# Routing attention with a gated feed-forward on one core: the cluster masks of the later steps on VectorE, and weight chunks loaded two ahead

## The chip, the core and the metric

The kernel runs on one core of a Trainium2 chip. A core has five engines with instruction streams of their own: TensorE (PE), which multiplies matrices out of SBUF into the banks of PSUM, VectorE (DVE), ScalarE (ACT), GpSimd (POOL) and SyncE (SP), which here issues the transfers. They wait for each other by semaphores alone, and each works its own stream in order. The metric is the device time of one execution in microseconds (us), the median over several runs.

## What is computed

The reference has two parts. Attention with a mask by clusters, for 4 batches and 8 heads of 768 positions and 64 features:

```python
q_assign = np.argmax(np.einsum('bhsd,hcd->bhsc', q_n, c_n), axis=-1)   # 16 clusters
k_assign = np.argmax(np.einsum('bhsd,hcd->bhsc', k_n, c_n), axis=-1)
mask = q_assign[:, :, :, None] == k_assign[:, :, None, :]
scores = scale * np.matmul(q, k.transpose(0, 1, 3, 2))
scores = np.where(mask, scores, -1000000000.0)
...
attn = attn / (np.sum(attn, axis=-1, keepdims=True) + 1e-09)
return np.matmul(attn, v).astype(np.float32)
```

Its result, as 3072 tokens of 512 features, goes through a feed-forward with 2048 hidden units:

```python
h = x @ w_in
relu6 = np.clip(h + 3.0, 0.0, 6.0)
g = h * relu6 / 6.0
return (g @ w_out).astype(np.float32)
```

The weights come as 64-bit floats; the kernel makes 32-bit ones of them.

## The kernel before

Two heads make a pair, 16 pairs in all (g = 0 to 15). A pair has 12 steps: two halves of the queries (hf) times six chunks of 128 keys (j). So there are 192 steps, numbered n; `where(n)` gives (g, hf, j). A batch is 4 pairs, 48 steps.

**One step.** `scores` (L425) writes, for both heads, keys by queries into a tile ps of two PSUM banks (two such tiles, L147). `scores_part` (L414) issues two matmuls, one for each head, first with the one-hot clusters xm (bf16; the keys' one-hots are inverted and scaled by -2^60, so that pairs of different clusters get -2^60), then with xf, the transposed queries and keys in fp32, which add the products. An fp32 matmul is two PE instructions in the profile, a bf16 one is one. At the first step of a pair xf goes first. `exponentials` (L438) is one ACT instruction from ps to ex in SBUF; `key_sums` (L456) adds ex to acc on POOL; `attn_v` (L468) multiplies by the values into pv, over six steps, and copies pv out to num. `divide` (L486) sums acc over the keys by a matmul with ones into pd, takes its reciprocal on DVE (L499), multiplies num (L500) and sends num to DRAM (L503), from where the feed-forward reads it. pd, like other small PSUM tiles (`scratch`, L174), is in the pool psum_t, which has one buffer from step 96 on.

**Masks on VectorE.** `masks`, `clusters`, `spread` and `by_vector` (L373 to L454) are a second way, for pairs from MASKED on. MASKED is 16 (L169), the number of pairs, so it is never taken.

**Preparing a pair.** `turn` (L303) transposes q and k in three parts, `cluster_scores` (L319) and `route` (L330) find the clusters (L337 and L343 on DVE), `route_turn` (L361) transposes the one-hots into xm. `prep_items` (L785) spreads this over the 12 steps of the pair before.

**Weights.** There are 32 chunks (L205 to L256). `load_weights` (L205) loads one into a raw tile (two buffers, L144); `decoding_steps` (L210) has five steps: split, join, power, rest and total, with two ACT instructions (L221, L237) and five on DVE (L225 to L252). split of chunk i asks for chunk i + 1 (L215); rest (L247) reads raw last. `share` (L815) says how many decoding steps follow each pair of steps. They run until about step 96.

**Feed-forward.** `ffn_items` (L602) has, for each block of 256 tokens, eight up items and seven down items. An up item (`halved`, L650) is a form with seven products instead of eight: PE writes three products into uX and four into uY (both from the pool psum_m with two buffers, L150), DVE adds them up (L669, L676), ACT lifts (L523), and DVE clips (L526) one item later (`finish`, L634). Every second item POOL makes sums of the gates (L648). A down item is eight matmuls of 256 (16 PE instructions, L693), with a few additions on DVE (L700).

**The order of the work.** The instructions stand in each engine's stream as the code issues them (`manual_schedule`, L879); nothing is reordered. The loop (L898) takes two steps at a time; r = n mod 12. Until step 96 each pair of steps is followed by values of earlier steps, preparation, decoding, and from step 60 on a few up items. From step 96 on (DECODED) the function `four_by_four` (L842) works four steps together: at r = 0, 4 and 8 two steps are followed by the values of four earlier steps, at r = 2, 6 and 10 by a slot of feed-forward items and preparation. `items_by` (L821) sets how many items are issued up to a step: four or five a slot. `divide` comes at r = 4 ahead of the values (for the second half of the pair before) and at r = 8 in the midst of the values (L865 to L871). `later` and `checks` defer small work: num's transfer and the range sums on ACT (L512, L513) are issued in the pair of steps after.

The items in the slots from step 118 on, U for up and D for down: 118 UUUU, 122 UUUU, 126 DDDDD, 130 DDUU, 134 UUUUU, 138 UDDD, 142 DDDDU, 146 UUUU, 150 UUUD, 154 DDDDD, 158 DUUU, 162 UUUUU, 166 DDDD, 170 DDDU, 174 UUUUU, 178 UUDD, 182 DDDDD, 186 UUUU.

## Time and profile before

| what | value |
| --- | --- |
| median of 8 runs | 1014.46 us (1012.98 to 1018.86) |
| the profiled execution | 1016.26 us, of them 1014.4 us span |
| mean granted TensorE clock | 0.996 |
| busy share of the span: PE, DVE, ACT, POOL | 98%, 56%, 38%, 42% |
| score matmuls with xm (L418, bf16) | 384 instructions, 61.0 us busy |
| score matmuls with xf (L418, fp32) | 768 instructions, 157.0 us busy |
| reciprocals (L499) | 32, mean 2557 ns |
| bytes read from and written to HBM | 75.79 MB, 15.73 MB |

How to read the profile: it is one execution, recorded by the hardware, and all times in it are counted from the span's start. The span is from the first to the last instruction; the time of an execution has a little around it. PE is the matmul itself, PEld the load of its weights, which runs beside other matmuls. Matmuls overlap: the next begins before the last has drained, so the distance from start to start tells what one costs. A group line gives an engine, an operation, what it writes and reads with shapes, the number of instructions, their busy time and mean, and then the time that the engine was idle just ahead of them and who ended it. A timeline line has the start, the length, the engine and the group; in brackets is the idle time ahead of it. An arrow "<-" before an engine's name means "released by".

The trace can be cut by what the loop does. The first exponentials of the pairs stand at 15.0 us (pair 0), 111.9 (4), 139.7 (5), 244.2 (8, step 96), 313.8 (9), 380.6 (10, step 120), 717.6 (15); from 785 us on there is only feed-forward.

### The profile page before, as it was taken

What the parts mean: (1) busy time and instruction counts of PE and PEld (TensorE: products, weight loads), DVE (VectorE), ACT (ScalarE), POOL (GpSimd) and SP (SyncE); (2) the same over time, 40 slices, a digit from 0 to 9 for tenths busy, and PEclk for the clock granted to TensorE, in tenths of its full rate; (3) what the DMA queues carried; (4) which work ended last, traced back from release to release, by engine and by line L of the source; (5) the groups of instructions that cost most, each with busy time, mean ns of one, the idle gap of its engine ahead of it and who ended that gap; (6) DMA issues with size and microseconds to landing.
All of it is one profiled execution on the core that took longest, in us unless ns stands there. A gap on an engine that the chain in (4) does not pass through costs nothing.

```text
span 1014.4 us, 16735 instructions
## 1 busy us (share of the span) xinstructions
PE 991.0 (98%) x6560; PEld 736.4 (73%) x6560; DVE 564.5 (56%) x1085; ACT 390.4 (38%) x764; POOL 430.7 (42%) x363
## 2 busy tenths in 40 slices
PE   8999999999999999999999999999999999999996
PEld 4444445555688777788787777778777899999995
DVE  4788888988855255236336237147156372727270
ACT  6788877665233233234323333333223020201010
POOL 3877766665416326426415426515426130303030
PEclk9999999999999999999999999999999999999998
DMA  6344455532253052223223225123023041414120
GB/s 177 104 114 135 127 164 146 138 116 59 102 167 86 9 144 78 55 78 88 72 84 99 47 68 135 28 76 102 21 91 92 31 144 39 128 51 117 53 63 25
DMA packets 87560, 92.70 MB, mean 91 GB/s; under 512 B 53936, under 2 KB 68272, under 8 KB 87472
## 3 DMA queue, kind: packets, MB, share of 16 engines
q1 hardware_dynamic: 87328, 91.51, 31.9%
q8 instruction: 54, 0.88, 0.4%
q14 instruction: 34, 0.28, 0.1%
q10 hardware_dynamic: 144, 0.03, 0.0%
HBM read 75.79 MB, written 15.73 MB: 90 GB/s over the span
## 4 chain that ended last, share of the span: by engine, by line
PE 87%; DVE 6%; ACT 4%; DMA 1%; issue 1%; SPq 0%; ACTq 0%; DVEq 0%
PE Y L693 16%; PE uY L658 15%; PE ps L418 13%; PE X L693 12%; PE uX L658 12%; PE pv L474 11%; PE pqk L310 2%; PE pd L495 2%; PE ph L613 2%; PE pcs L323 1%; DVE tx L580 1%; DMA raw<-in_moe_w_out_dram 1%; ACT ex L441 1%; PE po L367 1%; DVE rcp L499 1%
## 5 line engine op out<-in xcount | busy, mean ns | idle before, releaser
L464 POOL TENSOR_TENSOR acc<-acc,ex 128x768 f32<-128x768 f32 x128 | 241.8, 1889 | 132.3 <-ACT ex L441 125.6
L648 POOL TENSOR_TENSOR g_sb<-g_sb 128x256 f32<-128x256 f32 x176 | 127.5, 746 | 319.3 <-DVE g_sb L526 298.1
L441 ACT ACTIVATE ex<-ps 128x768 f32<-128x768 f32 x192 | 148.4, 805 | 85.0 <-PE ps L418 84.5
L523 ACT ACTIVATE sx<-g_sb,half_c 128x512 f32<-128x512 f32 x88 | 63.6, 722 | 268.3 <-DVE g_sb L669 268.3
L418 PE MATMUL ps<-xf 64*128 64x384 f32 x768 | 157.0, 487 | 0.8 <-ACT ex L441 0.8
L474 PE MATMUL pv<-ex,vt 128*64 128x384 f32 x768 | 141.1, 496 | 0.0
L700 DVE TENSOR_TENSOR y<-y,Y 128x256 f32<-128x256 f32 x48 | 20.2, 420 | 169.9 <-PE Y L693 169.1
L474 PEld LDWEIGHTS pv<-ex,vt 128*64 128x64 f32 x768 | 48.7, 136 | 82.4 <-issue 72.7
L499 DVE RECIPROCAL rcp<-pd 128x384 f32<-128x384 f32 x32 | 81.8, 2557 | 47.7 <-PE pd L495 46.8
L461 POOL TENSOR_TENSOR acc<-ex 128x768 f32<-128x768 f32 x32 | 59.6, 1864 | 100.8 <-ACT ex L441 100.7
L658 PE MATMUL uX<-xb,w_in_sb 128*128 128x128 f32 x704 | 93.0, 275 | 0.0
L693 PE MATMUL X<-w_out_sb,g_sb 128*128 128x256 f32 x384 | 90.6, 384 | 0.0
L693 PE MATMUL Y<-T,g_sb 128*128 128x256 f32 x384 | 87.3, 380 | 0.0
L693 PE MATMUL Y<-w_out_sb,g_sb 128*128 128x256 f32 x384 | 87.2, 380 | 0.0
L658 PEld LDWEIGHTS uX<-xb,w_in_sb 128*128 128x128 f32 x704 | 85.7, 192 | 0.0
L418 PEld LDWEIGHTS ps<-xf 64*128 64x128 f32 x768 | 67.7, 188 | 21.7 <-issue 18.0
L693 PEld LDWEIGHTS X<-w_out_sb,g_sb 128*128 128x128 f32 x384 | 71.9, 192 | 13.8 <-issue 4.1
L693 PEld LDWEIGHTS Y<-T,g_sb 128*128 128x128 f32 x384 | 72.3, 190 | 11.2 <-issue 1.7
L693 PEld LDWEIGHTS Y<-w_out_sb,g_sb 128*128 128x128 f32 x384 | 72.2, 190 | 11.1 <-issue 1.1
L526 DVE SCALAR_TENSOR_TENSOR g_sb<-sx,g_sb 128x512 f32<-128x512 f32 x88 | 67.3, 770 | 0.9 <-ACT sx L523 0.9
L418 PE MATMUL ps<-xm 64*128 64x384 bf16 x384 | 61.0, 327 | 6.4 <-ACT ex L441 3.3
L669 DVE TENSOR_TENSOR g_sb<-uY,sx 128x128 f32<-128x128 f32 (+1 forms) x176 | 65.6, 414 | 0.1
(110 smaller groups left out, 1383.4 us busy)
## 6 DMA issues: line engine op xcount, KB each, us to landing
tx<-td SPq DMA_DIRECT2D x86, 384.0 KB, 3.2
raw<-in_moe_w_in_dram SPq DMA_DIRECT2D x16, 512.0 KB, 3.9
raw<-in_moe_w_out_dram SPq DMA_DIRECT2D x16, 512.0 KB, 3.6
qk<-in_q_dram SPq DMA_DIRECT2D x32, 192.0 KB, 4.3
qk<-in_k_dram SPq DMA_DIRECT2D x32, 192.0 KB, 4.7
vt<-in_v_dram SPq DMA_DIRECT2D x32, 192.0 KB, 3.8
xd<-num SPq DMA_DIRECT2D x32, 192.0 KB, 3.0
xb<-xd SPq DMA_DIRECT2D x12, 512.0 KB, 4.1
```

The lines of the kernel that those rows point to most:

```text
L418: nc.tensor.matmul(st["ps", n][:, t, 0:HALF], lhsT=x[r, NCH + j], rhs=x[r, hf * NHC : (hf + 1) * NHC], start=first, stop=last,)
L441: nc.scalar.activation(out=ex, in_=sc, func=ACT.Exp, scale=SM_SCALE)
L461: nc.gpsimd.tensor_tensor(out=acc, in0=st["ex", n - 1], in1=ex, op=ALU.add)
L464: nc.gpsimd.tensor_tensor(out=acc, in0=acc, in1=ex, op=ALU.add)
L474: nc.tensor.matmul(pv[t * D : (t + 1) * D], lhsT=vt[:, t, j], rhs=ex[:, t], start=(j == 0), stop=(j == NCH - 1),)
L499: nc.vector.reciprocal(out=rcp, in_=pd)
L523: nc.scalar.activation(out=r, in_=h, func=ACT.Relu, bias=half_c, scale=1.0 / 6.0)
L526: nc.vector.scalar_tensor_tensor(out=g, in0=r, scalar=1.0, in1=h, op0=ALU.min, op1=ALU.mult)
L648: eng.tensor_tensor(out=out_, in0=in0, in1=in1, op=op)
L658: nc.tensor.matmul(dst, lhsT=w[:, kt], rhs=x(kt), start=(kt == 0), stop=(kt == HK - 1))
L669: nc.vector.tensor_tensor(out=out_, in0=in0, in1=in1, op=ALU.add)
L693: nc.tensor.matmul(bank[:, half * HC : (half + 1) * HC], lhsT=g_sb[:, kind, i], rhs=w[:, i], start=(first and i == 0), stop=(last and i == ...
```

## The change

Pairs 10 to 15 (steps 120 to 191) now take the second way, and that way is another: `masks` writes 0 or -2^60 with a `tensor_scalar` on DVE straight into the banks of ps, out of xm (which now holds each query's cluster number on every partition) and the key's cluster number kid; PE then adds the score products onto it. The two masks of a step are written as soon as the exponentials two steps earlier have left the banks: at r = 0, 4 and 8 for the next two steps, four masks at once, ahead of the reciprocal; at r = 2, 6 and 10 singly, two behind a feed-forward item, from the first item on at r = 2, from the second on at r = 6 and 10. `clusters` now gives the numbers of queries and keys by two multiplications, one reduction and one copy, at the end of the slot at r = 6; `spread` transposes each number, repeated 128 times, in two parts instead of three. At r = 2, 6 and 10 the key sums follow their exponentials at once. The division is split: `sum_up` issues pd's matmuls right behind the last values of a half (r = 0 and 8, no longer r = 4 and 8), and the reciprocal and the multiplication follow at the end of that pair of steps. Only the division of step 95 stays at r = 4. Chunks are asked for two ahead, with three raw buffers, and `share` has one step more at r = 2 in the first part and one less at r = 4 in the second.

The diff, cut where only names or the index of `number` change:

```diff
@@ -141,7 +141,7 @@
     dram = pool("dram", 1, space=bass.MemoryType.DRAM)
     yp = pool("yp", 1)
     decoding = ctx.enter_context(ExitStack())
-    rawp = decoding.enter_context(tc.tile_pool(name="rawp", bufs=2))
+    rawp = decoding.enter_context(tc.tile_pool(name="rawp", bufs=3))
     decp = decoding.enter_context(tc.tile_pool(name="decp", bufs=2))
     startp = decoding.enter_context(tc.tile_pool(name="startp", bufs=1))
     psum_s = pool("psum_s", 2, space=PSUM)
@@ -166,7 +166,7 @@
     counts = const.tile([P, 2, NPAIR], F32, name="counts")
     w_low = const.tile([P, 1], F32, name="w_low")
-    MASKED = NPAIR
+    MASKED = NPAIR // 2 + 2
     st = {}
     later = []
     numbers = []
@@ -212,7 +212,7 @@
         got = {}
         def split():
-            load_weights(i + 1)
+            load_weights(i + 2)
             raw = st.pop(("raw", i))
             got.update(lo=raw[:, :, 0], hi=raw[:, :, 1])
             got["size"] = decp.tile([P, WC], BF16, name="wsize")
@@ -356,7 +357,7 @@
         later.append(count)
         if g >= MASKED:
-            numbers.append(lambda: clusters(g))
+            numbers.extend(clusters(g))
     def route_turn(g, part):
         if part == 0:
@@ -374,33 +375,36 @@
         return where(n)[0] >= MASKED
     def clusters(g):
-        oh = one_hot.rearrange("p j (t c) -> p j t c", t=2)[:, :, :, 0:C]
-        which = rtp.tile([P, NC2, 2, C], BF16, name="which")
-        nc.vector.tensor_tensor(
-            out=which, in0=oh, in1=number.unsqueeze(1).unsqueeze(1).to_broadcast([P, NC2, 2, C]), op=ALU.mult
-        )
+        oh = one_hot.rearrange("p (h j) (t c) -> p h j t c", h=2, t=2)[:, :, :, :, 0:C]
+        which = rtp.tile([P, 2, NCH, 2, C], BF16, name="which")
         qid = st["qid"] = rtp.tile([P, NCH, 2], BF16, name="qid")
-        kid = st["kid", g] = kidp.tile([P, NCH, 2], F32, name="kid")
-        nc.vector.tensor_reduce(out=kid, in_=which[:, NCH:], axis=AX.X, op=ALU.add)
-        nc.vector.tensor_scalar(
-            out=kid, in0=kid, scalar1=-1.0, scalar2=C * (C - 1) / 2.0, op0=ALU.mult, op1=ALU.add
-        )
-        qsum = rtp.tile([P, NCH, 2], F32, name="qsum")
-        nc.vector.tensor_reduce(out=qsum, in_=which[:, 0:NCH], axis=AX.X, op=ALU.add)
-        nc.vector.tensor_copy(out=qid, in_=qsum)
-    def spread(g, part):
-        if part == 0:
+        kid = st["kid", g] = kidp.tile([P, 2, NCH, 2], F32, name="kid")
+        def weigh():
+            for h in range(2):
+                nc.vector.tensor_tensor(
+                    out=which[:, h], in0=oh[:, h],
+                    in1=number[:, h].unsqueeze(1).unsqueeze(1).to_broadcast([P, NCH, 2, C]), op=ALU.mult,
+                )
+        def collect():
+            nc.vector.tensor_reduce(out=kid, in_=which, axis=AX.X, op=ALU.add)
+        def narrow():
+            nc.vector.tensor_copy(out=qid, in_=kid[:, 0])
+        return [weigh, collect, narrow]
+    def spread(g, t):
+        if t == 0:
             st["xm", g] = xp.tile([P, NC2, P], BF16, name="xm")
-        pb = scratch([P, 4, P], "pb")
-        for i in range(4):
-            t, j = divmod(4 * part + i, NCH)
-            nc.tensor.matmul(
-                pb[:, i], lhsT=st["qid"][:, j, t : t + 1].to_broadcast([P, P]), rhs=ident_q,
-                start=True, stop=True,
-            )
-        nc.scalar.copy(out=st["xm", g][:, 4 * part : 4 * part + 4], in_=pb)
+        pb = scratch([P, NCH, P], "pb", BF16)
+        for j in range(NCH):
+            nc.tensor.transpose(
+                out=pb[:, j], in_=st["qid"][:, j, t : t + 1].to_broadcast([P, P]), identity=ident_q
+            )
+        nc.scalar.copy(out=st["xm", g][:, t * NCH : (t + 1) * NCH], in_=pb)
     def where(n):
@@ -409,48 +413,53 @@
     def scores_qk(n):
         st["ps", n] = psum_s.tile([P, 2, 512], F32, name="ps")
-        scores_part(n, st["xf", where(n)[0]], True, by_vector(n))
-    def scores_part(n, x, first, last):
+        scores_part(n, st["xf", where(n)[0]], True, False)
+    def scores_part(n, x, first, last, onto=False):
         g, hf, j = where(n)
         for t in range(2):
             r = slice(t * D, (t + 1) * D)
             nc.tensor.matmul(
                 st["ps", n][:, t, 0:HALF], lhsT=x[r, NCH + j],
                 rhs=x[r, hf * NHC : (hf + 1) * NHC], start=first, stop=last,
+                skip_group_check=onto,
             )
     def scores(n):
         g, hf, j = where(n)
+        if by_vector(n):
+            scores_part(n, st["xf", g], False, True, True)
+            return
         if ("ps", n) not in st:
-            if hf == j == 0 or by_vector(n):
+            if hf == j == 0:
                 scores_qk(n)
             else:
                 st["ps", n] = psum_s.tile([P, 2, 512], F32, name="ps")
                 scores_part(n, st["xm", g], True, False)
                 scores_part(n, st["xf", g], False, True)
                 return
-        if not by_vector(n):
-            scores_part(n, st["xm", g], False, True)
+        scores_part(n, st["xm", g], False, True)
     def exponentials(n):
         sc = st.pop(("ps", n))[:, :, 0:HALF]
         ex = st["ex", n] = expp.tile([P, 2, HALF], F32, name="ex")
         nc.scalar.activation(out=ex, in_=sc, func=ACT.Exp, scale=SM_SCALE)
-    def masks(n):
+    def masks(n, heads=(0, 1)):
         g, hf, j = where(n)
-        if not by_vector(n):
+        if n >= total or not by_vector(n):
             return
-        ex = st["ex", n]
-        for t in range(2):
-            nc.vector.scalar_tensor_tensor(
-                out=ex[:, t].rearrange("p (a b) -> p a b", b=P),
+        if ("ps", n) not in st:
+            st["ps", n] = psum_s.tile([P, 2, 512], F32, name="ps")
+        for t in heads:
+            nc.vector.tensor_scalar(
+                out=st["ps", n][:, t, 0:HALF].rearrange("p (a b) -> p a b", b=P),
                 in0=st["xm", g][:, t * NCH + hf * NHC : t * NCH + (hf + 1) * NHC],
-                scalar=st["kid", g][:, j, t : t + 1], in1=ex[:, t].rearrange("p (a b) -> p a b", b=P),
-                op0=ALU.is_equal, op1=ALU.mult,
+                scalar1=st["kid", g][:, 1, j, t : t + 1], scalar2=-FAR,
+                op0=ALU.not_equal, op1=ALU.mult,
             )
     def key_sums(n):
@@ -484,6 +493,9 @@
     def divide(n):
+        return sum_up(n)()
+    def sum_up(n):
         g, hf, _ = where(n)
         b, kt = divmod(g, NKT)
         if kt == 0 and hf == 0:
@@ -495,17 +507,21 @@
             nc.tensor.matmul(
                 pd[t * D : (t + 1) * D], lhsT=ones, rhs=acc[:, t], start=True, stop=True
             )
-        rcp = nump.tile([P, HALF], F32, name="rcp")
-        nc.vector.reciprocal(out=rcp, in_=pd)
-        nc.vector.tensor_tensor(out=num, in0=num, in1=rcp, op=ALU.mult)
-        def keep():
-            nc.sync.dma_start(st["xd", b][:, kt, hf * HALF : (hf + 1) * HALF], num)
-            in_range(2 * g + hf, rcp)
-            if (kt, hf) == (NKT - 1, 1):
-                later.append(lambda: (waiting.extend((b, m) for m in range(NHC)), load_block()))
-        return keep
+        def inverse():
+            rcp = nump.tile([P, HALF], F32, name="rcp")
+            nc.vector.reciprocal(out=rcp, in_=pd)
+            nc.vector.tensor_tensor(out=num, in0=num, in1=rcp, op=ALU.mult)
+            def keep():
+                nc.sync.dma_start(st["xd", b][:, kt, hf * HALF : (hf + 1) * HALF], num)
+                in_range(2 * g + hf, rcp)
+                if (kt, hf) == (NKT - 1, 1):
+                    later.append(lambda: (waiting.extend((b, m) for m in range(NHC)), load_block()))
+            return keep
+        return inverse
     def in_range(i, rcp):
@@ -789,7 +805,7 @@
         turns = [lambda part=part: turn(g, part) for part in range(3)]
         one_hots = [lambda: route_turn(g, 0), lambda: route_turn(g, 1)]
         if g >= MASKED:
-            one_hots = [lambda part=part: spread(g, part) for part in range(3)]
+            one_hots = [lambda t=t: spread(g, t) for t in range(2)]
         scores_of = [lambda: cluster_scores(g)]
         ways = [lambda: route(g)]
         if fours:
@@ -815,8 +831,8 @@
     def share(n, r):
         if n < READY:
-            return {0: 4, 2: 2, 4: 3, 6: 1, 8: 2, 10: 4}[r]
-        return {0: 6, 2: 5, 4: 5, 6: 3, 8: 5, 10: 5}[r]
+            return {0: 4, 2: 3, 4: 3, 6: 1, 8: 2, 10: 4}[r]
+        return {0: 6, 2: 5, 4: 4, 6: 3, 8: 5, 10: 5}[r]
     def items_by(n):
@@ -827,7 +843,7 @@
     HOLD = 6
     st["early"] = st["free"] = True
     st["last"] = False
-    fill, checks, unmasked = [], [], []
+    fill, checks, singles = [], [], []
     st["done"], st["valued"] = 0, DECODED - lag_v
     def check_all():
@@ -845,36 +861,40 @@
         if r % 4 == 2:
             for i in steps:
                 exponentials(i)
-            unmasked.extend(steps)
+            for i in steps:
+                key_sums(i)
             check_all()
-            for op in numbers:
-                op()
-            numbers.clear()
+            for t in range(2):
+                singles.extend(lambda i=i, t=t: masks(i, [t]) for i in (n + 2, n + 3))
             return
         for i in steps[: 1 if r == 8 else 2]:
             exponentials(i)
         check_all()
-        for i in unmasked:
-            masks(i)
-            key_sums(i)
-        unmasked.clear()
-        if r == 4 or n >= total:
-            m = n - r % per_pair - 1 if n < total else total - 1
-            if ("acc", *where(m)[:2]) in st and m < st["valued"]:
-                later.append(divide(m))
-                ready(m)
+        for i in steps[: 1 if r == 8 else 2]:
+            masks(i + 2)
+        inverse = None
+        if n == DECODED + 4:
+            inverse = sum_up(DECODED - 1)
+            ready(DECODED - 1)
         for i in range(st["valued"], min(n, total)):
             attn_v(i)
-            if i % per_pair == NCH - 1:
-                later.append(divide(i))
+            if i % NCH == NCH - 1 and i != DECODED - 1:
+                inverse = sum_up(i)
+                ready(i)
         st["valued"] = min(n, total)
         for i in steps[1 if r == 8 else 2 :]:
             exponentials(i)
+        for i in steps[1 if r == 8 else 2 :]:
+            masks(i + 2)
         for i in steps:
-            masks(i)
             key_sums(i)
+        if inverse:
+            later.append(inverse())
     with tc.manual_schedule():
         nc.scalar.dma_start(cen, centroids.rearrange("h c d -> (h c) d"))
@@ -888,6 +908,7 @@
         centroid_turn()
         nc.vector.tensor_copy(out=ident_q, in_=ident)
         load(1, "q", "k")
+        load_weights(1)
         cluster_scores(0)
         scores_qk(0)
         route(0)
@@ -929,6 +950,15 @@
                         fill.pop(0)()
                     if i < len(prep):
                         prep[i]()
+                    for _ in range({6: 2 * (i > 0), 10: 2 * (i > 0)}.get(r, 2)):
+                        if singles:
+                            singles.pop(0)()
+                if fours:
+                    for op in singles + numbers:
+                        op()
+                    singles.clear(), numbers.clear()
             if r == 6 and fours:
                 load(g + 2, "q", "k")
                 load(g + 1, "v")
```

## The prediction

> **What bounds the kernel now.** First the page's shares and its chain of work:
> ```profile
> PE 991.0 (98%) x6560; PEld 736.4 (73%) x6560; DVE 564.5 (56%) x1085; ACT 390.4 (38%) x764; POOL 430.7 (42%) x363
> ...
> PE 87%; DVE 6%; ACT 4%; DMA 1%; issue 1%; SPq 0%; ACTq 0%; DVEq 0%
> ```
> TensorE (PE) is the chain. A busy share is an average, so I asked the stage that the masks change for itself, in the view by stretches (five whole pairs of the interleaved stage; columns are length, then busy us and count by engine):
> ```profile
> 380.60:717.60 337.00, 335.91 (x2303) 259.27 (x2303) 148.42 (x326) 113.29 (x207) 148.93 (x128) 1.00 0.28 77
> ```
> PE is busy 335.91 of 337.00 us at full clock, VectorE (DVE) 148 of them. So there a microsecond of PE work removed is a microsecond of time, unless PE starts to wait. What one step's mask costs is in the timeline of a step pair (start, length):
> ```profile
> 603.38 0.34 PE L418 MATMUL ps<-xm 64*128 64x384 bf16 x2
> ...
> 603.56 0.81 PE L418 MATMUL ps<-xf 64*128 64x384 f32 x4
> ...
> 604.20 0.33 PE L418 MATMUL ps<-xm 64*128 64x384 bf16 x2
> ...
> 604.36 0.81 PE L418 MATMUL ps<-xf 64*128 64x384 f32 x4
> ```
> Lengths overlap; the pace is start to start: the mask's two matmuls hold PE 0.16 to 0.18 us, the scores' four 0.64. Over the trace a mask matmul's median pace is 0.0805 us, 0.161 a step.
>
> Then whether DVE has room where the masks go, between feed-forward "up" items (PE: 12 matmuls into uX, 16 into uY at 0.112 us, 3.14 us an item):
> ```profile
> 621.75 0.29 DVE L669 TENSOR_TENSOR sx<-uY,sx 128x128 f32<-128x128 f32 x1 [0.84 <-PE uY L658]
> 621.96 0.75 DVE L669 TENSOR_TENSOR g_sb<-uY,sx 128x128 f32<-128x128 f32 x2
> 622.62 0.68 DVE L526 SCALAR_TENSOR_TENSOR g_sb<-sx,g_sb 128x512 f32<-128x512 f32 x1
> 623.41 0.29 DVE L676 COPY sx<-uX 128x128 f32<-128x128 f32 x1
> 623.73 0.62 DVE L669 TENSOR_TENSOR sx<-uX,sx 128x128 f32<-128x128 f32 x2
> 624.91 0.29 DVE L669 TENSOR_TENSOR sx<-uY,sx 128x128 f32<-128x128 f32 x1 [0.56 <-PE uY L658]
> ```
> In a run of up items DVE works 2.6 of 3.16 us: from 621.75 without rest to 624.35, idle 0.56. At 624.35 uX's bank is free, and PE wants it at 624.60 (its next weight load): 0.25 us of slack.
>
> **The masks, gain.** Steps 120 to 191, 72 of them, lose two mask matmuls each: 72 x 0.161 = 11.6 us of PE. Nothing hides this gain: PE is full there. The four score matmuls stay. One-hot transposes (12 a pair, L367, 56 ns apart) become 12 transposes of a repeated column, with two ACT copies as before. A weight load from a repeated column is in no row; the bf16 one-hot load takes 98 ns beside matmuls 56 ns apart, an fp32 load 190 ns. Bounds: 0, and 72 x (190 - 56) = 9.6 us. I take 0, since shape and type are those of the nearer row.
>
> **The masks, cost on DVE.** 144 instructions, bf16 in SBUF to fp32 in PSUM, 384 wide. The nearest row is L225, also a tensor_scalar from SBUF into PSUM:
> ```profile
> L225 DVE TENSOR_SCALAR wtop<-raw x32: 681/695/716, 12.6 to 227.5; 128x512 uint32<-128x512 uint32 x32
> ```
> With L676 (128 wide, 291 ns) an element costs (695 - 291)/384 = 1.05 ns, so 384 take 0.56 us. Independent DVE instructions overlap a little (621.75 + 0.29 is past 621.96), so I space masks 0.50 us. Lower bound 0.40, the elements alone; upper 1.14, what the multiplication L500 takes on average when POOL is running (0.56 when it isn't).
>
> The Trainium skill (VectorE: DVE Perf Modes, "The DRAIN you can't avoid") speaks against my spacing: the next operation starts only when the pipeline is empty. The rows above show starts 0.08 us before the previous end. By the rule masks would be 0.56 apart and the sum below some 3 us worse.
>
> In all 144 x 0.5 = 72 us go to DVE, which has over half its time free, so only places count. A group of 12 steps has three slots of filling; each is followed by a step pair whose four masks come at once.
>
> *Masks at once.* At the step pair from 515.62 the last up item's lift and the two exponentials keep ACT until 518.14 and 518.84. Masks start at 518.2, are done for the third step at 519.3 and for the fourth at 520.3. PE without the mask matmuls: two scores to 517.0, 16 value matmuls to 519.7, third step 519.7 to 520.35, fourth at 520.35. Just covered. Where the division now stands in between (first and third step pair of a group) PE's pd adds 0.64 us of cover. I charge 0.1 us for the six middle ones: 0.6. Cover gone, each extra 0.1 us of a mask costs 0.4 us there.
>
> *Masks between fill items.* Two masks behind an item push the copy out of uX by 1.0 us against 0.25 of slack: the item after next starts 0.75 late; a second pair behind it costs 0.5, because DVE then no longer waits its 0.56. (Check: route at L337/L343 puts 1.2 us there now, against 0.33 us of PE transposes, and PE waits 0.59, 0.66 and 0.33 us at 549.7, 617.2 and 684.8.) The items follow from items_by (L821): the slots at 118, 150 and 186 have one such pair followed by enough up items, 162 and 174 two; slots of "down" items have none, their DVE work is two 0.42 us additions in 3.46. 7 pairs x 0.5 to 0.75: 4.4. The slots at 122, 134, 146 and 158 carry transposes of the next pair (0.44 us of PE each) behind the same items: 7 pairs x 0 to 0.3, 1.0.
>
> *The division.* Reciprocal 2.56 and multiplication 0.56 to 1.75 us now come behind the four masks, about 2 us later than now, and reach into the next slot's first up item. Nearly always a turn's or a spread's transposes cover this; 0 to 0.5 us in two slots (118, 178): 0.5. The wait queued behind is DVE's own: everything of the slot.
>
> *Cluster numbers.* Two multiplications (0.35 each as L343), a reduction (0.55 as L337), a copy (0.15): 1.4 us, six times, on DVE ahead of the third step pair's masks; ACT's lift and exponential run meanwhile and pd's 0.64 us follows. Nothing; 1 us each if that cover goes. 16 more POOL memsets at 0.1 us end long before its first sum at 18 us. Key sums issued earlier on POOL keep their number: nothing.
>
> Stalls: 0.6 + 4.4 + 1.0 + 0.5 = 6.5 us.
>
> **The chunks.** ACT's wait for a raw chunk shows twice, 2.02 us and this:
> ```profile
> 226.87 0.67 ACT L221 ACTIVATE wsize<-raw 128x512 bf16<-128x512 f32 x1 [4.87 <-DMA raw<-in_moe_w_out_dram]
> ```
> A chunk is asked for when DVE has done with the one before last (SP's own wait on L247) and lands 3.6 us later, just when ACT wants it. A third buffer asks one chunk, 3.5 us or more of DVE work, earlier; both waits end, and SP's queue is less often blocked ahead of qk loads. PE waits on their account 1.04 us (for xf at 142.69) and 1.88 (for ex at 230.47): 2.9. Bounds: 2.9 gained, 1 lost, since one decode step moves from step pair 4 to 2. I take 2.5: DVE and ACT stay nearly full in those pairs.
>
> **Sum.** -11.6 - 2.5 + 6.5 = -7.6 us. The profiled execution took 1016.26 us (span 1014.4, 1.9 around it), so 1008.7 for one like it. It lay 1.8 us over the median of the runs, 1014.46; I forecast the median: **1006.9**.
>
> **Rivals.**
> *All of it hidden.* Masks of 0.40 us, no stall: -11.6 - 2.9 = -14.5, 1000. For: DVE has 190 of 337 us idle. Against: 0.25 us of slack per up item.
> *The wait is only exchanged.* Masks of 0.65 to 0.75, or slow repeated-column loads (+9.6): near 0, 1011 to 1017. Break-even: from 0.56 each further 0.1 us costs 2.4 (six middle step pairs) + 14 x 0.2 = 5.2 us; the 7.6 are gone at about 0.7.
> *DVE becomes the bound, slower.* One mechanism: a mask waits for POOL's sums as L500 does and takes 1.14 us. Then the fourth mask comes 518.2 + 4.6 = 522.8, 2.4 us late in six step pairs, 1.8 in twelve with pd; fill pairs 14 x 1.2 more: 14 + 22 + 17 = 53 us more than forecast, 1060. It decides from 0.7 us a mask. For: POOL sums run at that moment. Against: L225 stays at 695 beside a running POOL; it reads one SBUF tensor, L500 two.
> *It doesn't do what it says.* Only as exchange, above; the division's new place alone is worth nothing, since PE doesn't wait for it in this stage.
>
> **Chances.** Forecast (1002 to 1011) 0.50; hidden (under 1002) 0.17; exchanged 0.16; slower 0.17. Range 1000 to 1018: it leaves out the far end of the slow case and a little below. 0.2%, 2 us, is about what a measurement tells from no change: faster, below 1012.4: 0.50 + 0.17 + 0.04 = 0.71; within 0.2% 0.08; slower 0.17 + 0.04 = 0.21.
>
> **What would show it.** The mask group's mean (0.56), its idle-before on ACT; score matmuls on xm down from 384 to 240; PE waits on DVE before ps scores (none or 0.1) and before uX in runs of up items (0.5 to 0.75 each at slots 150, 162, 174, 186); ACT's DMA waits at L221 gone. I am wrong if the mask group's mean is over 0.7, if pb transposes are further apart than 56 ns, or if DVE's lag reaches the scores in all 18 step pairs.

## The result, and the profile after

After the change the median is **1009.98 us** (1008.30 to 1012.17, 17 runs) beside 1014.57 us of the kernel before (46 runs). The ratio is **0.995, 95% interval 0.9941 to 0.996**: 4.6 us faster. The forecast was 1006.9, 7.6 us faster. The profiled execution took 1009.93 us, 1008.1 of them span, so the traces differ by 6.3 us.

The page of the kernel after, its shares and its chain of work:

```profile
PE 985.3 (98%) x6416; PEld 729.7 (72%) x6416; DVE 655.2 (65%) x1253; ACT 390.7 (39%) x764; POOL 431.8 (43%) x379
...
PE 73%; DVE 5%; ACT 1%; issue 1%; ACTq 0%
```

PE lost the 144 mask matmuls, DVE won 168 instructions and 91 us, and PE is still busy 98% of the span. The parts of this chain add up to 80% only, so it was not followed through all of its steps, and nothing is read from it here. The stretch of pairs 10 to 14, from first exponential to first exponential, in the view by stretches (same columns as before):

```profile
378.62:712.60 333.98, 332.00 (x2181) 254.89 (x2179) 220.57 (x466) 113.76 (x206) 146.20 (x126) 1.00 0.28 79
```

The five pairs took 337.00 us before and 333.98 now; PE is still busy for all but 2 us of them, DVE for 221 us in place of 148. Below I compare from pair 9's first exponential to the end, which holds all of the masks' work: **700.5 us before, 696.5 after**. The mask group and its nearest row, in the groups and the view by source line:

```profile
L458 DVE TENSOR_SCALAR ps<-xm,kid 128x384 f32<-128x384 bf16 x144 | 83.7, 616 | 26.4 <-ACT ex L449 23.2
```

```profile
L225 DVE TENSOR_SCALAR wtop<-raw x32: 681/695/714, 12.3 to 224.3; 128x512 uint32<-128x512 uint32 x32
```

A mask takes 0.616 us, not 0.56. A step pair (the middle one of pair 13), in the timeline after:

```profile
599.30 1.56 PE L422 MATMUL ps<-xf 64*128 64x384 f32 x8
...
600.79 2.80 PE L483 MATMUL pv<-ex,vt 128*64 128x384 f32 x16
601.09 1.49 ACT L449 ACTIVATE ex<-ps 128x768 f32<-128x768 f32 x2
601.91 2.45 DVE L458 TENSOR_SCALAR ps<-xm,kid 128x384 f32<-128x384 bf16 x4 [0.95 <-ACT ex L449]
603.52 1.90 PE L422 MATMUL ps<-xf 64*128 64x384 f32 x8
604.53 1.74 ACT L449 ACTIVATE ex<-ps 128x768 f32<-128x768 f32 x2 [1.96 <-PE ps L422]
605.36 0.85 PE L324 MATMUL pcs<-xf,cnT 128*32 128x384 f32 x8
```

Start to start, the first block of scores (the eight matmuls of two steps) holds PE 600.79 - 599.30 = 1.49 us. Before, the same block with its mask matmuls held it 1.72, from 603.38 in the lines of the prediction to the next group:

```profile
605.10 0.87 PE L495 MATMUL pd<-acc,ones 128*64 128x384 f32 x4
```

The second block of after takes 605.36 - 603.52 = 1.84: its last mask ends at 604.36, in the middle of it. Four masks take 2.45 us, so one starts (2.45 - 0.616) / 3 = 0.61 us behind the other on average. But four masks issued singly, in a slot, take less:

```profile
706.80 2.18 DVE L458 TENSOR_SCALAR ps<-xm,kid 128x384 f32<-128x384 bf16 x4
```

These stand (2.18 - 0.616) / 3 = 0.52 us apart. The difference goes with the order: four at once write both masks of one step and then both of the next, the single ones go from step to step. By the order of the code, of the 90 masks that directly follow another the 36 that write into the same tile ps start 0.64 to 0.66 us behind it, the 54 that write into the other tile 0.52 to 0.53. And between up items:

```profile
617.45 0.68 DVE L542 SCALAR_TENSOR_TENSOR g_sb<-sx,g_sb 128x512 f32<-128x512 f32 x1
...
618.04 1.13 DVE L458 TENSOR_SCALAR ps<-xm,kid 128x384 f32<-128x384 bf16 x2
...
619.09 0.28 DVE L692 COPY sx<-uX 128x128 f32<-128x128 f32 x1
...
620.07 0.52 PEld L674 LDWEIGHTS uX<-xs,tx 128*128 128x128 f32 x4 [0.36 <-DVE sx L685]
```

DVE goes from the clip of one item straight to two masks and on to the copy out of uX; the next item waits 0.36 us at its first weight load. (Another pair of masks, 3.5 us earlier, costs 0.17 in the same way.) ACT's wait for raw chunks, in the groups by line, first before and then after, is gone:

```profile
L221 ACT ACTIVATE wsize<-raw 128x512 bf16<-128x512 f32 x32 | 21.9, 684 | 6.9 <-DMA raw<-in_moe_w_out_dram 6.9
```

```profile
L221 ACT ACTIVATE wsize<-raw 128x512 bf16<-128x512 f32 x32 | 21.8, 682 | 0.0
```

The 72 transposes of a repeated column stand 56 ns apart, like the one-hot transposes: they cost nothing more.

### The profile page after: what moved, and what is told of

Read it like the earlier page. It is cut to its first block, busy times and chain, and to the rows that moved or that the text cites. A ratio compares the mean times of both kernels' runs of the same rounds, so it can differ in the third digit from the quotient of the medians.

```text
span 1008.1 us, 16657 instructions
## 1 busy us (share of the span) xinstructions
PE 985.3 (98%) x6416; PEld 729.7 (72%) x6416; DVE 655.2 (65%) x1253; ACT 390.7 (39%) x764; POOL 431.8 (43%) x379
## 4 chain that ended last, share of the span: by engine, by line
PE 73%; DVE 5%; ACT 1%; issue 1%; ACTq 0%
PE Y L709 17%; PE uY L674 14%; PE X L709 12%; PE uX L674 11%; PE ps L422 8%; PE pv L483 7%; PE pqk L311 1%; PE pd L507 1%; PE ph L629 1%; DVE sx L685 1%; PE pcs L324 1%; DVE g_sb L685 1%; DVE ps L458 1%; DVE T L563 1%; DVE rcp L513 0%
## 5 line engine op out<-in xcount | busy, mean ns | idle before, releaser
L458 DVE TENSOR_SCALAR ps<-xm,kid 128x384 f32<-128x384 bf16 x144 | 83.7, 616 | 26.4 <-ACT ex L449 23.2
L685 DVE TENSOR_TENSOR g_sb<-uY,sx 128x128 f32<-128x128 f32 (+1 forms) x176 | 65.7, 414 | 0.3 <-DVE g_sb L685 0.3
L542 DVE SCALAR_TENSOR_TENSOR g_sb<-sx,g_sb 128x512 f32<-128x512 f32 x88 | 64.5, 738 | 1.4 <-ACT sx L539 1.4
```

Source lines behind the costliest of these rows:

```text
L458: nc.vector.tensor_scalar(out=st["ps", n][:, t, 0:HALF].rearrange("p (a b) -> p a b", b=P), in0=st["xm", g][:, t * NCH + hf * NHC : t * NC ...
L542: nc.vector.scalar_tensor_tensor(out=g, in0=r, scalar=1.0, in1=h, op0=ALU.min, op1=ALU.mult)
L685: nc.vector.tensor_tensor(out=out_, in0=in0, in1=in1, op=ALU.add)
```

## The experiments

Two measures are used. A median has its ratio to the kernel before as it was measured beside it, with the 95% interval. Inside a trace, times are taken from pair 0's first exponential, since that one itself stands anywhere from 14.4 to 16.8 us, in kernels whose work up to there differs little. Cut there, pairs 0 to 7 repeat within 0.1 us between kernels that share their work, and the stretch from pair 9 on, in four kernels without masks on DVE, took 699.6 to 699.9 us; the trace of before, with 700.5, lies 0.8 above these, mostly behind PE's last matmul (7.8 us to the end of the span there, 7.1 to 7.5 in the four). Pair 8 moves by 1.5 us, for a reason that the last section shows.

### Each part by itself

`chunks_alone` is the kernel before with three raw buffers, chunks asked for two in advance, and the new shares. `order_chunks` is the kernel after with MASKED = 16, so without masks on DVE. `masks_alone` is the kernel after with the three edits on chunks undone. `no_masks` is the kernel after in which steps 120 to 191 have no masks at all.

The edits of `chunks_alone`, which `masks_alone` undoes:

```diff
-    rawp = decoding.enter_context(tc.tile_pool(name="rawp", bufs=2))
+    rawp = decoding.enter_context(tc.tile_pool(name="rawp", bufs=3))
-            load_weights(i + 1)
+            load_weights(i + 2)
+        load_weights(1)
-            return {0: 4, 2: 2, 4: 3, 6: 1, 8: 2, 10: 4}[r]
-        return {0: 6, 2: 5, 4: 5, 6: 3, 8: 5, 10: 5}[r]
+            return {0: 4, 2: 3, 4: 3, 6: 1, 8: 2, 10: 4}[r]
+        return {0: 6, 2: 5, 4: 4, 6: 3, 8: 5, 10: 5}[r]
```

Those of `order_chunks` and, in `scores` and `masks`, of `no_masks`:

```diff
-    MASKED = NPAIR // 2 + 2
+    MASKED = NPAIR
```

```diff
-            scores_part(n, st["xf", g], False, True, True)
+            if ("ps", n) not in st:
+                st["ps", n] = psum_s.tile([P, 2, 512], F32, name="ps")
+            scores_part(n, st["xf", g], True, True)
...
-        if n >= total or not by_vector(n):
+        if True:
             return
```

> The kernel before with only the chunks part of the change: three raw buffers, chunks asked for two ahead, the changed share of decoding steps. Theory 1 (as predicted): both DMA waits of ACT end and 2.5 us with them, 1012. Rival (from the two traces: step 96 is reached at 244.2 us before and 244.4 after though ACT's DMA waits of 6.9 us are gone): the waits are exchanged for waits on VectorE, which is nearly full there; 0, 1014.5.

> The changed kernel with the masks left to TensorE in all pairs (MASKED = 16): the chunks and the new place of divisions and key sums remain. Theory 1 (the new order is worth nothing by itself): the time of the run with the chunks alone, within 0.5 us. Rival (pair 8 of the changed kernel took 67.15 us in place of 69.66 and holds no mask on VectorE): the order gives 2 to 2.5 us below the run with the chunks alone.

> The changed kernel with the chunks part undone (two raw buffers, one ahead, the old share). Theory 1: the masks give 11.6 less 6.5 of stalls, 5.1, and the chunks' 2.5 are missing: 1009.5, and 2.5 over the changed kernel. Rival (chunks worth nothing): the time of the changed kernel, 1010.

> The changed kernel without any mask in steps 120 to 191: this part of the computation is left out, TensorE and VectorE both save it. It shows what the changed kernel would take if no mask ever made TensorE wait. Theory 1 (a step's mask costs TensorE 0.161 us, 11.6 in all; of it 6.5 are lost to stalls): 6.5 below the changed kernel, 1003.5. Rival (from the changed kernel's trace: two steps' scores take 1.49 us in place of 1.72, because the fp32 matmuls that now come first cost 0.1 more; so 8.8 us are gained and about 4.4 lost to stalls): 4.4 below, 1005.5.

| kernel | median us | ratio to before | pairs 0 to 7 | pair 8 | pair 9 to the end |
| --- | --- | --- | --- | --- | --- |
| before | 1014.57 | | 229.2 | 69.7 | 700.5 |
| after | 1009.98 | 0.995 (0.9941 to 0.996) | 229.8 | 67.2 | 696.5 |
| chunks_alone | 1011.99 | 0.9978 (0.9965 to 0.999) | 229.8 | 66.9 | 699.6 |
| order_chunks | 1013.07 | 0.9985 (0.9972 to 0.9998) | 229.8 | 67.2 | 699.9 |
| masks_alone | 1010.79 | 0.9958 (0.9944 to 0.9972) | 229.2 | 69.8 | 696.4 |
| no_masks | 1003.73 | 0.9895 (0.9881 to 0.991) | 229.8 | 67.1 | 690.9 |

In the traces the two parts lie in different stretches and add up. (By the medians, `masks_alone` and `chunks_alone` multiply to 0.9936 beside 0.995 of after; their intervals are too wide to tell.) The masks work from pair 9 on: taking the mask matmuls away without putting anything in their place brings 699.9 - 690.9 = **9.0 us**, not 11.6; putting DVE's masks in costs 696.5 - 690.9 = **5.6 us**, where the prediction had 6.5. So the rival of `no_masks` was right on the gain, and the cost lies between its 4.4 and the 6.5. What is left of the masks is 3.4 us. The order by itself is worth nothing in the traces (699.9 beside 699.6); the median of `order_chunks` is 1.1 us over that of `chunks_alone`, with intervals that overlap. The chunks bring 1.8 us in the trace, but not where the prediction put them: pairs 0 to 7 get 0.6 us longer although ACT's waits are gone, and pair 8 gets 2.5 us shorter.

### Why a block without mask matmuls saves too little

A block loses 1.719 - 1.490 = 0.229 us, where the pace of four mask matmuls is 4 x 0.0805 = 0.32. `xf_first` puts nothing away and only turns the order in the kernel before:

```diff
-            if hf == j == 0 or by_vector(n):
-                scores_qk(n)
-            else: ...   # xm first, xf second
+            scores_qk(n)   # xf first, xm second
```

> The kernel before, with the fp32 matmul of xf ahead of the bf16 matmul of xm in every step (before has it so only in a turn's first step); the matmuls are the same ones. Theory: the first matmul of a block of scores that follows another tile shape costs 0.10 us more if it is fp32 and 0.02 if it is bf16, which is why a block without its mask matmuls saves 0.23 us and not 0.32. Then the 35 two-step blocks from the pair 9 to the end take 1.82 us instead of 1.72, that stretch 704.0 instead of 700.6, and the whole kernel 4 to 8 us longer than before (the blocks of the earlier steps pay as well). Rival: what is missing from the gain is something else in the blocks, for instance waiting for a mask: then the blocks keep 1.72 us, and the time is that of before within 1 us.

It took 1019.71 us, ratio 1.005 (1.0034 to 1.0065): 4.7 us slower than before, which had 1014.99 beside it. Every one of the 36 blocks from step 120 on takes 1.815 or 1.816 us, where 30 of them took 1.719; pair 9 to the end takes 703.0 us, 3.1 to 3.4 over the four kernels named above (35 x 0.097 = 3.4). In the timeline of `xf_first`:

```profile
605.50 0.92 PE L418 MATMUL ps<-xf 64*128 64x384 f32 x4
606.25 0.33 PE L418 MATMUL ps<-xm 64*128 64x384 bf16 x2
606.41 0.81 PE L418 MATMUL ps<-xf 64*128 64x384 f32 x4
607.05 0.33 PE L418 MATMUL ps<-xm 64*128 64x384 bf16 x2
607.31 0.87 PE L489 MATMUL pd<-acc,ones 128*64 128x384 f32 x4
```

The first group of xf, which follows another tile shape, takes 0.92 us; the second, behind xm, 0.81. So the theory of the run holds in its numbers: whichever type comes first in a block pays, fp32 0.10 us and bf16 hardly anything. The mask matmuls had stood in front and hid that. 30 blocks save 0.229 and the 6 that had xf first already 0.326: 8.8 us, near the 9.0 measured. What in PE makes the first fp32 matmul dearer, the change of tile shape or something else, the runs don't tell.

### The masks that come late

`pcs_early` moves the cluster scores of the next pair (pcs) from behind the blocks at r = 6 to ahead of them:

```diff
+            if fours and prep and r == 6:
+                prep.pop(0)()
             if fours:
                 four_by_four(n, r, steps)
-            if prep and r == (6 if fours else 4):
+            if prep and not fours and r == 4:
```

> The kernel after, with the cluster scores of the next pair put ahead of the step pair that starts at the seventh step of a group, and not behind its first items, so that the last of four masks has some 0.65 us more of PE work in front of it. Theory: the five blocks of scores there that take 1.77 to 1.83 us do so because they wait for that fourth mask; then they take 1.5, and the time is 1.5 to 2 us below after (1008.3). Rival: they are long because of what runs on PE just before, or the wait only moves to the next consumer: then nothing, within 0.5 us of after.

It took 1008.18 us, ratio 0.9936 (0.9922 to 0.9951; after has 0.995). In the trace, pair 9 to the end takes 694.9 us, 1.65 less than after. The timeline at the place shown above:

```profile
598.11 2.80 PE L483 MATMUL pv<-ex,vt 128*64 128x384 f32 x16
598.40 1.49 ACT L449 ACTIVATE ex<-ps 128x768 f32<-128x768 f32 x2
599.22 2.45 DVE L458 TENSOR_SCALAR ps<-xm,kid 128x384 f32<-128x384 bf16 x4 [0.95 <-ACT ex L449]
600.84 0.85 PE L324 MATMUL pcs<-xf,cnT 128*32 128x384 f32 x8
601.62 1.56 PE L422 MATMUL ps<-xf 64*128 64x384 f32 x8
...
603.11 0.71 PE L674 MATMUL uX<-xs,tx 128*128 128x128 f32 x4
```

The masks come as late as in after against the values (1.11 us behind pv's start, 1.12 in after), but PE has pcs to do first; the block takes 603.11 - 601.62 = 1.49. All five blocks fell to 1.49 us; in after, four of them had taken 1.83 and one 1.77. So they did wait for the fourth mask.

### Double masks

`masks_twice` writes each mask twice.

```diff
-        for t in heads:
+        for t in [t for t in heads for _ in range(2)]:
```

> The kernel after, with each mask written twice by VectorE into the same bank. Theory of the prediction: masks are on the path where four come at once and where they stand between up items, 5.2 us for each further 0.1 us; a second mask 0.61 us behind the first adds 0.61 x 52 = 32 us (1042), most of it in waits of the scores of the six middle step pairs and of uX. Rival, from the trace of after: only some 5.6 us of stalls are there, most masks have cover to spare, and the price is well under that: 10 to 15 us (1020 to 1025). Rival that VectorE isn't on the path at all: under 3 us.

It took 1078.53 us, ratio 1.0655 (1.061 to 1.07): 69 us more than after. That is twice what my rate gave and far from the rivals. The waits of PE, in us, times and longest:

```profile
PE ps L422 <- DVE ps L458: 37.8, 31, 1.7
PE uX L674 <- DVE sx L685: 15.7, 20, 1.7
```

With 1.23 us a mask, the scores wait 31 times and not only in the six middle step pairs: all 18 blocks that follow four masks take 2.9 to 4.2 us, also those with pd (0.64 us) in front. The rate of 5.2 us for 0.1 us a mask left those out, and holds only near the forecast's mask; the prediction's slower rival, which counted them, had 53 us for 0.58 us more a mask. A further part is the clock, the share of TensorE's full clock that is granted: in this stage it falls again and again, here in the second of three stretches of 4 us (last columns: clock, DMA share, GB/s):

```profile
640.00:644.00 4.00, 1.92 (x12) 0.49 (x8) 3.82 (x7) 0.81 (x1) 3.92 (x5) 1.00 0.00 0
644.00:648.00 4.00, 3.45 (x15) 1.17 (x16) 0.41 (x1) 1.29 (x2) 2.13 (x2) 0.60 0.00 0
648.00:652.00 4.00, 4.00 (x37) 4.00 (x37) 1.68 (x6) 0.00 (x0) 0.74 (x1) 0.97 0.12 10
```

PE was busy 1.92 of 4 us, and right behind that it is granted 0.60. There are six such falls from 376 us to PE's last matmul, each to 0.50, of 3.41 us or twice that (675.52 to 682.35); half of their 23.9 us, 12 us, is lost. The waits at ps, uX and X (37.8, 15.7 and 1.3 us) and the clock make 67 of the 70.2 us by which pair 9 to the end is longer; the rest is not accounted for. So the price of a late mask can be more than the wait for it.

### What the chunks bring

`buffers_alone` is the kernel before with the third buffer and the earlier requests, but the old shares; `share_alone` has the new shares alone; `after_oldshare` is the kernel after with the old shares.

```diff
-            return {0: 4, 2: 3, 4: 3, 6: 1, 8: 2, 10: 4}[r]
-        return {0: 6, 2: 5, 4: 4, 6: 3, 8: 5, 10: 5}[r]
+            return {0: 4, 2: 2, 4: 3, 6: 1, 8: 2, 10: 4}[r]
+        return {0: 6, 2: 5, 4: 5, 6: 3, 8: 5, 10: 5}[r]
```

> The kernel before, with three raw buffers and chunks asked for two in advance, and the shares of decoding of before. Theory that the buffers bring the gain: pair 8 takes 66.9 us as with both parts (69.7 in before) and the time is 2 to 2.5 us below before. Rival, that the changed shares bring it: pair 8 takes 69.7, and the time is that of before within 1 us, since the waits on DMA that end here had cover on PE.

> The kernel before with the new shares of decoding and nothing else (two raw buffers, one chunk in advance). Theory: the shares cost by themselves, since the decode step that moves into the slot of the third step comes in front of work that PE needs, so about 3 to 4 us are lost with any number of buffers: 1017 to 1019. Rival: the shares cost only because three buffers let VectorE run ahead into them; with two, ACT's wait for the chunk sets the pace, and the time is that of before within 1 us.

> The kernel after with one part undone: the shares of decoding are those of before, while the three raw buffers and the masks stay. Theory, from the two runs on the chunks (three buffers alone gained 6 us, buffers with the new shares 2.4): the new shares cost 2.8 us in pairs 0 to 7 and 1.4 in pair 8, so the time from the first exponential to the end falls by 4.2 us against after, and the median by 3 to 4, to 1006 to 1007. Rival: in after the lost time comes from elsewhere (the order of the division), and the shares matter only with the old order: then 1009.5 to 1010.5.

| kernel | raw buffers | shares | median us | ratio to before | pairs 0 to 7 | pair 8 |
| --- | --- | --- | --- | --- | --- | --- |
| before | 2 | old | 1014.57 | | 229.2 | 69.7 |
| share_alone | 2 | new | 1012.63 | 0.9988 (0.9974 to 1.0001) | 229.9 | 67.2 |
| chunks_alone | 3 | new | 1011.99 | 0.9978 (0.9965 to 0.999) | 229.8 | 66.9 |
| buffers_alone | 3 | old | 1008.78 | 0.9939 (0.9926 to 0.9952) | 227.0 | 65.5 |
| after_oldshare | 3 | old, masks | 1005.63 | 0.9916 (0.9901 to 0.9931) | 227.0 | 65.5 |

`buffers_alone` gains by itself as much as the whole change (0.9939 beside 0.995, with intervals that overlap), over twice what its theory expected, and `after_oldshare` is 4.4 us below after; its interval doesn't meet that of after. My expectation for `share_alone`, a loss, was wrong: by themselves the new shares end one wait and make another (pair 8 is 2.5 us shorter, pairs 0 to 7 are 0.7 longer; the interval of the median just holds 1). The theory behind it, that a decode step moved into an earlier slot costs, was wrong too. The waits show what happens. Before, at the head of pair 8, and then in `buffers_alone` at the same work:

```profile
272.05 1.51 PE L323 MATMUL pcs<-xf,cnT 128*32 128x384 f32 x8 [2.52 <-DVE rcp L499]
```

```profile
268.95 0.85 PE L323 MATMUL pcs<-xf,cnT 128*32 128x384 f32 x8
```

From step 96 on pcs and pd share the one buffer of psum_t, so pcs waits for the reciprocal, and DVE reaches that late because the decoding before it was late. With three buffers DVE has no lag left, and the wait is gone. `xf_first` agrees: with two buffers and the old shares, but PE 2.9 us later by step 96, that wait is 0.5 us and pair 8 took 66.6. With the new shares the decoding ends one slot earlier, so it is early enough even with two buffers, but then the weight sums (L547, for the form with seven products) follow in that slot. DVE in `share_alone`, then in `buffers_alone`:

```profile
231.02 5.47 DVE L547 TENSOR_TENSOR T<-w_out_sb 128x1024 f32<-128x1024 f32 x2
236.41 2.82 DVE L547 TENSOR_TENSOR T<-w_out_sb,T 128x1024 f32<-128x1024 f32 x1
239.16 2.54 DVE L499 RECIPROCAL rcp<-pd 128x384 f32<-128x384 f32 x1
```

```profile
232.70 1.66 DVE L247 SCALAR_TENSOR_TENSOR wunit<-raw,wunit 128x512 f32<-128x512 uint32 x1
234.40 0.69 DVE L252 TENSOR_TENSOR w_out_sb<-wtop,wunit 128x512 f32<-128x512 f32 x1
235.12 1.99 DVE L547 TENSOR_TENSOR T<-w_out_sb 128x1024 f32<-128x1024 f32 x1
237.04 2.55 DVE L499 RECIPROCAL rcp<-pd 128x384 f32<-128x384 f32 x1
```

Between the one-hots and the reciprocal stand three weight sums in the first, 8.1 us, and two decoding steps and one weight sum in the second, 4.3 us. The share counts both as three steps. PE's transposes of one-hots wait for that reciprocal, 1.83 us in `share_alone`, `chunks_alone` and after, none with the old shares and three buffers. So the third buffer was worth 6.3 us in the trace, and the changed shares took 4.2 of them back: 2.8 in pairs 0 to 7, 1.8 of them with that wait, and 1.4 in pair 8, by the clock behind it (last section). In `pcs_early` and `masks_twice`, which have the wait but no fall of the clock there, pair 8 took 65.7 and 65.5.

### The versions that go further

`best` is the kernel after with the old shares, pcs moved as in `pcs_early`, and the queries' cluster numbers summed straight into bf16 (the copy is gone). `best9` is that with MASKED = 9.

```diff
-            nc.vector.tensor_reduce(out=kid, in_=which, axis=AX.X, op=ALU.add)
+            nc.vector.tensor_reduce(out=kid[:, 1], in_=which[:, 1], axis=AX.X, op=ALU.add)
-            nc.vector.tensor_copy(out=qid, in_=kid[:, 0])
...
+                nc.vector.tensor_reduce(out=qid, in_=which[:, 0], axis=AX.X, op=ALU.add)
```

> The kernel after with three edits: shares of before, the cluster scores ahead of the step pair at the seventh step, and the cluster numbers of the queries summed straight into bf16 (the copy, 0.17 us alone and up to 1.8 beside a running POOL, is gone). If the terms add: 1010.0 - 3.2 - 1.7 - 0.5 = 1004.6. Rival, that the gains overlap or the copy's time moves into the sum: 1006 to 1007.

> The kernel of the run best, with VectorE's masks from pair 9 on and not from pair 10 (84 steps and not 72). Theory: a pair with masks gains 1.5 us of PE and loses 0.4 to 0.9, so this is 0.6 to 1 us below best; the stretch of pair 9 is shorter by that. Rival: the division of the first batch and the weight sums keep VectorE busier in pair 9, masks come late there, and the time is that of best or up to 1 us longer.

`best` took 1004.01 us, ratio 0.9899 (0.9882 to 0.9915), `best9` **1002.74 us, ratio 0.9884 (0.9868 to 0.9901)**. Both beat after; the terms of `best` added up, to within 0.6 us. The copy was worth looking at because of this, in after:

```profile
555.16 1.82 POOL L473 TENSOR_TENSOR acc<-acc,ex 128x768 f32<-128x768 f32 x1
555.20 1.80 DVE L395 CAST qid<-kid 128x12 bf16<-128x12 f32 x1
...
556.92 2.44 DVE L458 TENSOR_SCALAR ps<-xm,kid 128x384 f32<-128x384 bf16 x4
...
559.51 0.92 PE L422 MATMUL ps<-xf 64*128 64x384 f32 x4 [0.32 <-DVE ps L458]
```

Without the copy the two stretched blocks at that place fall from 2.08 us (pair 12) and 1.82 (pair 13) to 1.52 and 1.68. That is 0.7 us. Pair 9 to the end is only 0.15 us shorter than in `pcs_early` (694.7 beside 694.9), but up to PE's last matmul it is 0.6 shorter: the rest lies behind that matmul, where 7.7 us follow in `best` and 7.3 in `pcs_early`, and where all the traces here have between 7.0 and 7.8. `best9` is 1.1 us shorter than `best` from pair 9 on and 0.6 longer in pair 8; the intervals of the two overlap, so which is better stays open.

## Why the prediction was right in sign, and where its sizes failed

- **The bound** held: PE was the chain, and where PE work fell away without a new wait, time fell by the same amount (`no_masks`: 8.8 us by the blocks, 9.0 by the stretch).
- **Masks, gain, 72 x 0.161 = 11.6.** Mis-sized: 9.0. The step "a mask matmul's pace, times their number" takes the matmuls out of a row in which they also stood in front of an fp32 matmul; `xf_first` shows the 0.10 us a block that shows once they are gone. The trace of before had it: blocks with xf first took 1.816 us, the others 1.719.
- **A mask, 0.56 us, 0.50 apart.** Measured 0.616; the nearest row gave the duration within 10%. The distance is 0.52 where masks go from one tile ps to the other, near the prediction's, and 0.65 where the second follows the first into the same tile, which makes 0.61 on average in four at once. The rule of the Trainium skill that the prediction set against itself (VectorE: DVE Perf Modes, "The DRAIN you can't avoid") would put the full 0.616 between any two, by estimate; it fits the average of the fours and not the masks between items. The same section adds that an operation that is not held starts earlier; what holds the second mask of a tile back, no run here shows. POOL does not lengthen a mask: 605 to 624 ns over all 144, so the slower rival's mechanism is absent.
- **Masks at once, 0.6.** Measured 2.7 us of stretched score blocks: five at r = 6 by 0.28 to 0.34 us each (shown by `pcs_early`), two by 0.9 together behind the late cluster numbers, the rest 0.1. "Just covered" became "just not", as the prediction's own rate, 0.4 us for each 0.1 us of a mask, has it.
- **Masks between items, 4.4 + 1.0, and the division, 0.5.** The remaining 5.6 - 2.7 = 2.9 us, under half of the prediction. Added up start to start from pair 9 on, the groups of PE that write uX and uY take 265.7 us in after and 262.9 in `no_masks`, so 2.8 of it lies in the up items, as forecast; before uX PE waits seven times, 0.4 us at most where the prediction had 0.5 to 0.75. The 0.25 us of slack were read at one item that came behind a run without rest. That DVE's idle time of 0.5 to 0.85 us at most items took up the rest is argued from the timeline, not tried.
- **Cluster numbers, nothing.** Nearly: in one of six groups the 0.17 us copy took 1.80 beside POOL. Without the copy (`best`), 0.7 of the 0.9 us just named are gone.
- **Chunks, 2.5.** The sum was near (1.8 in the trace; 2.4 by the medians of `chunks_alone`), its account wrong, so the nearness is luck. The waits on DMA ended as forecast, and pairs 0 to 7 were 2.2 us shorter for it where the shares stayed (`buffers_alone`). What the prediction missed is the 2.5 us wait of pcs for the reciprocal, worth 4.1 us, since its view of waits looked at ACT's DMA alone; and it bounded the changed shares by 1 us, where they cost 4.2 beside three buffers.
- **The errors cancelled in part**: 2.6 us less gain, 0.9 less stall. The median fell 1.7 us less than the traces, which is their scatter: 1008.3 to 1012.2 in one kernel. None of the signs of being wrong that the prediction named came.

## What to carry to other kernels

Before counting a removed instruction by its pace, look for the same block without it in the trace: what follows may cost more once it stands first. When a wait ends, look through all waits of the bounding engine for the next one on the same chain, and give shares of background work in microseconds, not in steps. Work put on an idle engine is free only while each place has cover; an order that puts independent PE work ahead of the consumer buys that cover for nothing.

## What the runs showed of the hardware

**A wait of PE can be paid twice.** Behind the 1.83 us wait at 240.1 us in after, the clock granted was below one; in `pcs_early`, with the same wait, it was not. Both kernels in stretches of 4 us:

```profile
241.00:245.00 4.00, 2.98 (x18) 1.39 (x17) 3.97 (x5) 2.48 (x6) 0.10 (x1) 0.80 0.60 186
245.00:249.00 4.00, 4.00 (x22) 1.56 (x20) 4.00 (x5) 1.92 (x4) 0.15 (x1) 0.77 0.00 0
```

```profile
241.00:245.00 4.00, 3.06 (x22) 1.43 (x23) 3.97 (x5) 2.55 (x6) 0.02 (x1) 1.00 0.61 186
245.00:249.00 4.00, 4.00 (x25) 2.29 (x22) 4.00 (x5) 2.96 (x5) 0.23 (x1) 1.00 0.00 0
```

The two together give (0.20 + 0.23) x 4 / 0.5 = 3.4 us at half clock, and a narrower stretch shows it:

```profile
243.42:246.83 3.41, 3.41 (x14) 1.37 (x16) 3.41 (x4) 2.60 (x6) 0.00 (x0) 0.50 0.24 86
```

It cost 1.7 us. It came in five of the seven traces with that wait (not in `pcs_early` and `masks_twice`), and at the end of pcs' 2.5 us wait in before (0.50 from 271.94 to 275.35), where it makes 1.6 of the 4.1 us that pair 8 had to give. The Trainium skill (TensorE: Matmul & The Clock Gate, "HAM oscillation — how this bites in real kernels") warns of PE idle for more than about 3.4 us; here 1.83 us were enough, but not each time. Its "Part 1: The HAM clock gate" says that the window in which PE's activity is counted runs freely, which fits a fall that comes in some executions and not in others; that it is the cause, no run here shows.

**A small DVE copy beside POOL** took 1.80 us instead of 0.17 (lines above) and ended 0.02 us behind POOL's sum, while masks with the same neighbour kept their 0.61. Which of the two starts first matters: the 36 copies in six traces (after, `masks_alone`, `after_oldshare`, `pcs_early`, `no_masks`, `masks_twice`) have six that began during such a sum, and all six ended 0.02 to 0.03 us behind it, after 1.18 to 1.81 us; the other 30, among them those that began up to 0.1 us ahead of one, took 0.17. In `no_masks`:

```profile
688.30 1.82 POOL L475 TENSOR_TENSOR acc<-acc,ex 128x768 f32<-128x768 f32 x1 [1.17 <-ACT ex L451]
```

```profile
688.63 1.51 DVE L395 CAST qid<-kid 128x12 bf16<-128x12 f32 x1
```
